# Block sums, low parts and normalisation of a seven-product matrix multiply, moved between engines and in the queues

## The chip, the cores and the metric

The kernel runs on one core of a Trainium2 chip. The metric is the device time of one execution in microseconds, the median of several runs. The engines are TensorE (PE, with its weight loads PEld), VectorE (DVE), ScalarE (ACT), GpSimd (POOL) and SyncE (SP, which issues DMAs); each executes its own queue in order.

## The reference

Three stages in float32: attention with a bias from positions, a product of two projections with a third, and a last block. Only that last block is touched:

```python
h = x @ w_in                                  # 1152 x 512 by 512 x 1024
e = np.exp(h - np.max(h, axis=-1, keepdims=True))
sm = e / (np.sum(e, axis=-1, keepdims=True) + 1e-09)
solu = h * sm
mu = np.mean(solu, axis=-1, keepdims=True)
var = np.mean((solu - mu) ** 2, axis=-1, keepdims=True)
ln = (solu - mu) / np.sqrt(var + 1e-06) * g_ln
return ln @ w_out                             # 1024 x 512
```

The gains `g_ln` are multiplied into the rows of `w_out` ahead of time (tile `wo2`).

## The kernel before

**Split numbers.** A float32 product on TensorE is made of three products of rounded parts: each operand is split into a high part (ScalarE rounds it, type fp32r) and a low part (operand minus high part, one subtraction on VectorE or GpSimd). Names end in `h` or `hi` and `l` or `lo`.

**Units.** The 1152 rows are nine units of 128 rows, 0 to 8. For a unit, `proj(u)` multiplies its rows with `w_in` (24 matmuls of 512 columns, into `ph`, one of two PSUM buffers). `norm(u)` is a generator of four steps: (1) VectorE's maxima (L890, L891) and ScalarE's exponentials (L894); (2) the products `ev` (L897); (3) sums and statistics (L899 to L905), which end in a `pow` on GpSimd (L906); (4) VectorE's scale (L908) and the normalised `ev` (L909). `transposed(u)` turns `ev` on TensorE (L918, eight transposes, into two of the four `pl` PSUM buffers).

**Seven products.** The output product is made for two units at a time, as a 2 x 2 block product by seven block multiplications in place of eight. Of the weights `wo2` four block sums `t1` to `t4` are needed (`weights_sums`, in two halves, k = 0 and 2, each of four subtractions on GpSimd, L957, then four roundings to `th`, L960, and four low parts `tl` on GpSimd, L964). Of the rows of a pair `rows_sums(ua, ub)` makes the copies `raw` (L971), the four sums `s1` to `s4` (GpSimd, L977), the rounded plain blocks `a1` (L978, L979) and `a` (the tile `a22`, L980, L981), and the four rounded sums with their low parts, `s12` and `s34` (ScalarE L983, GpSimd L984). `seven(ua, ub)` is a generator of seven steps: each runs 12 matmuls of 256 columns into one of the same four PSUM buffers (`pa11b11`, `pa12b21`, `ps2t2`, `ps1t1`, `ps3t3`, `pa22t4`, `ps4b22`; the profile drops the last digit) and then adds the result in (L1009 on VectorE; the first result is copied to `part` by ScalarE, L1012). SyncE sends the finished rows (L945). Unit 8, the odd one, goes alone: `alone(8)` splits it, `final(8)` multiplies it (L936, `py`).

**Order.** There is no scheduler: the program text gives each engine its queue, and a generator's step is put where `next` is called. The loop over `todo` ends the second stage: it sums into `x2s` (L810), splits into `x2h` (L866) and `x2l` (L868; on GpSimd for the last four blocks), splits `wo2`, and starts unit 0 and the weights' sums. Then come the weights' sums and units 1 and 2, and then a loop over j = 0, 2, 4, which for each pair (j, j+1) runs `seven` between the projections and normalisations of units j+2 and j+3; in the last turn (`end`) unit 8 comes in too. Buffers: `nat` has four (the `t` sums, `s1` to `s4`, the result rows `osb` and `part`), `gh` and `gl` three each (`a1`, `s12`, `s34`, unit 8's split), `big` two (`x2s`, `wo2`, then `th`, `raw`).

Of the kernel before, what the change touches and what calls it, by code (L numbers as in the profile page):

```python
# [10 lines left out]
F32 = mybir.dt.float32  # L11
F32R = mybir.dt.float32r
I32 = mybir.dt.int32
AF = mybir.ActivationFunctionType
ALU = mybir.AluOpType
AX = mybir.AxisListType
PSUM = bass.MemoryType.PSUM
P = 128
# [32 lines left out]
def tile_kernel(ctx, tc, q, k, v, w1, b1, w2, w_a, w_b, w_out, w_in2, w_out2, g_ln, psi, rpsi, out):  # L51
    nc = tc.nc
# [16 lines left out]
    KF = FF2 // P  # L69
# [90 lines left out]
    with ExitStack() as actx:  # L160
# [426 lines left out]
        first, first_w = [], {}  # L587
# [361 lines left out]
    HN = DM // 2  # L949
    KH = KF // 2  # L950

    def weights_sums():
        for k in range(0, KH, 2):
            b11, b12, b21, b22 = (wo2[0][:, o * KH + k:o * KH + k + 2, n * HN:(n + 1) * HN] for o in range(2) for n in range(2))
            raw = [natp.tile([P, 2, HN], F32, tag="nat", name=f"t{i + 1}_{k}") for i in range(4)]
            for i, a, b in ((0, b12, b11), (1, b22, raw[0]), (2, b22, b12), (3, raw[1], b21)):
                nc.gpsimd.tensor_tensor(out=raw[i], in0=a, in1=b, op=ALU.subtract)  # L957
            yield
            for i in range(4):
                nc.scalar.copy(th[:, i, k:k + 2], raw[i])  # L960
                if i % 2:
                    yield
            for i in range(4):
                nc.gpsimd.tensor_tensor(out=tl[:, i, k:k + 2], in0=raw[i], in1=th[:, i, k:k + 2].bitcast(F32), op=ALU.subtract)  # L964

    blocks = {}

    def rows_sums(ua, ub):
        for k, u in enumerate((ua, ub)):
            for a, pl in transposed(u):  # L970
                nc.scalar.copy(raw[:, 2 * k + a], pl)  # L971
            yield
        r11, r12, r21, r22 = (raw[:, i] for i in range(4))
        (ah, al), (s12h, s12l), (s34h, s34l) = tiles = [[pools[0].tile([P, 2, 512], F32R, tag=f"g{t_}", name=f"{n}{t_}_{ua}") for t_ in "hl"] for n in ("a1", "s12", "s34")]
        s1, s2, s3, s4 = (natp.tile([P, 512], F32, tag="nat", name=f"s{i + 1}_{ua}") for i in range(4))
        for o, x, y, op in ((s1, r21, r22, ALU.add), (s2, s1, r11, ALU.subtract), (s3, r11, r21, ALU.subtract), (s4, r12, s2, ALU.subtract)):
            nc.gpsimd.tensor_tensor(out=o, in0=x, in1=y, op=op)  # L977
        nc.scalar.copy(ah, raw[:, 0:2])  # L978
        nc.vector.tensor_tensor(out=al, in0=raw[:, 0:2], in1=ah.bitcast(F32), op=ALU.subtract)  # L979
        nc.scalar.copy(a22[:, 0], r22)  # L980
        nc.vector.tensor_tensor(out=a22[:, 1], in0=r22, in1=a22[:, 0].bitcast(F32), op=ALU.subtract)  # L981
        for h, l, i, x in ((s12h, s12l, 1, s2), (s12h, s12l, 0, s1), (s34h, s34l, 0, s3), (s34h, s34l, 1, s4)):
            nc.scalar.copy(h[:, i], x)  # L983
            nc.gpsimd.tensor_tensor(out=l[:, i], in0=x, in1=h[:, i].bitcast(F32), op=ALU.subtract)  # L984
        view = lambda t: t.rearrange("p (c t) -> p c t", t=P)
        blocks[ua] = {n: tuple(view(t[:, i]) for t in pair) for n, pair, i in (("a11", tiles[0], 0), ("a12", tiles[0], 1), ("s1", tiles[1], 0), ("s2", tiles[1], 1), ("s3", tiles[2], 0), ("s4", tiles[2], 1))}
        blocks[ua]["a22"] = tuple(view(a22[:, i]) for i in range(2))
        yield

    def seven(ua, ub, last=False):  # L990
        A = blocks.pop(ua)
        B = {f"b{k + 1}{n + 1}": tuple(w[:, k * KH:(k + 1) * KH, n * HN:(n + 1) * HN] for w in (wo_h, wo_l)) for k in range(2) for n in range(2)}
        B.update({f"t{i + 1}": (th[:, i], tl[:, i]) for i in range(4)})
        oa, ob = (natp.tile([P, DM], F32, tag="nat", name=f"osb_{u}") for u in (ua, ub))
        tmp = natp.tile([P, DM], F32, tag="nat", name=f"part_{ua}")
        u2, u4 = tmp[:, 0:HN], tmp[:, HN:DM]

        def summed_block(a, b):
            ps = ps_l.tile([P, 512], F32, tag="l", name=f"p{a}{b}_{ua}")[:, 0:HN]
            (xh, xl), (wh, wl) = A[a], B[b]  # L1000
            i = 0
            for c in range(KH):
                for x, w in ((xh, wh), (xh, wl), (xl, wh)):
                    nc.tensor.matmul(ps, x[:, c], w[:, c], start=(i == 0), stop=(i == 3 * KH - 1))  # L1004
                    i += 1
            return ps

        def plus(o, x, y, op=ALU.add):
            nc.vector.tensor_tensor(out=o, in0=x, in1=y, op=op)  # L1009

        left, right = slice(0, HN), slice(HN, DM)
        nc.scalar.copy(u2, summed_block("a11", "b11"))  # L1012
        yield
        plus(oa[:, left], summed_block("a12", "b21"), u2)
        if last:
            sent(ua, oa, left)
        yield
        plus(u2, summed_block("s2", "t2"), u2)
        yield
        plus(u4, summed_block("s1", "t1"), u2)  # L1020
        yield
        p7 = summed_block("s3", "t3")
        plus(ob[:, right], p7, u4)
        plus(u2, p7, u2)
        yield
        plus(ob[:, left], u2, summed_block("a22", "t4"), ALU.subtract)
        sent(ub, ob, slice(0, DM))
        yield
        plus(oa[:, right], summed_block("s4", "b22"), u4)
        sent(ua, oa, right if last else slice(0, DM))  # L1030
        yield
# [5 lines left out]
    for j, (tg, d) in enumerate(todo):  # L1037
# [8 lines left out]
            nrm = norm(seq[0])  # L1046
        if nrm:
            next(nrm, None)
        if j == KF:
            ws = weights_sums()  # L1050
            next(ws)
    inputs(*todo[-1])
    octx.close()
    fb = ctx.enter_context(tc.tile_pool(name="fb", bufs=1, side="right"))
# [4 lines left out]
    every = lambda gen: [None for _ in gen]  # L1059
    proj(1)  # L1060
    every(nrm)
    next(ws)
    next(ws)
    second = norm(1)
    next(second)
    next(ws)
    proj(2)
    every(second)
    every(ws)
    raw = big.tile([P, 4, 512], F32, tag="big", name="raw")  # L1070
    rows = rows_sums(0, 1)
    next(rows)
    every(rows)
    one = nu - 1
    for j in range(0, one - 2, 2):
        a, b = j + 2, j + 3
        end = b == one - 1
        if j:
            proj(a)
            next(rows)  # L1080
        first = norm(a)
        next(first)
        if j:
            every(rows)
        if end:
            proj(one)
            next(first)
            mid = norm(one)
            next(mid)
        proj(b)  # L1090
        every(first)
        if end:
            next(mid)
        second = norm(b)
        next(second)
        f = seven(j, j + 1)
        next(f)
        next(f)
        if end:
            every(mid)  # L1100
        next(second)
        next(f)
        next(f)
        next(f)
        next(second)
        rows = rows_sums(a, b)
        if end:
            every(alone(one))
            next(rows)
        every(f)  # L1110
        every(second)
        if not end:
            next(rows)
    every(rows)
    final(one)
    every(seven(a, b, True))
# [43 lines left out]
```

## Time and profile before

| | us |
|---|---|
| median of 3 runs | 549.32 (547.86 to 550.11) |
| the profiled execution | 551.31 |
| its span, first to last instruction | 549.5 |
| TensorE busy | 506.7 (92%) |
| VectorE busy | 412.0 (75%) |
| ScalarE busy | 299.6 (55%) |
| GpSimd busy | 247.1 (45%) |

The mean granted TensorE clock is 0.975 of full speed. The code of the diff runs from about 404 us to the end of the span. Busy shares are means over three stages; what one stage is limited by is read from its own stretch. A wait is put down to what ended it last by the profile.

### The profile page before, as it was taken

The numbers are of one execution on the slowest core, as the hardware profiler recorded it, in microseconds if no ns is written. First come the engines' busy times: TensorE is split into PE (matmuls) and PEld (weight loads), VectorE is DVE, ScalarE is ACT, GpSimd is POOL, SyncE is SP. The second block draws the span as 40 slices with busy tenths as digits, with TensorE's granted clock in tenths as the row PEclk, the third lists the DMA queues.
The fourth block names the chain that finished last, engine by engine and source line by source line (L and its number), as shares of the span: only waits on it lengthen the run. The fifth ranks groups of instructions, "written<-read, shape, count | busy, mean of one in ns | idle before, by whom it ended". The sixth has DMA issues, their size and how long they took to land.

```text
span 549.5 us, 13771 instructions
## 1 busy us (share of the span) xinstructions
PE 506.7 (92%) x5546; PEld 456.5 (83%) x5546; DVE 412.0 (75%) x826; ACT 299.6 (55%) x643; POOL 247.1 (45%) x301
## 2 busy tenths in 40 slices
PE   7979999999989999999999999999999459878787
PEld 4548778878879999999999999999997358776677
DVE  4789999999867259789989889788546465566662
ACT  5789899999978245555533452343434431425131
POOL 2046676776868322222212224222477960806235
PEclk9999999999989999999999999999999788979989
DMA  8699654445621065454434344430000001010011
GB/s 163 167 202 206 138 126 106 108 106 135 170 70 41 2 192 154 125 160 143 149 116 151 118 120 149 151 118 1 2 1 0 0 1 38 1 39 1 0 39 57
DMA packets 63330, 51.76 MB, mean 94 GB/s; under 512 B 40990, under 2 KB 53539, under 8 KB 63268
## 3 DMA queue, kind: packets, MB, share of 16 engines
q1 hardware_dynamic: 62992, 50.88, 34.9%
q8 instruction: 43, 0.70, 0.6%
q14 instruction: 19, 0.16, 0.1%
q10 hardware_dynamic: 276, 0.02, 0.0%
HBM read 36.73 MB, written 2.36 MB: 71 GB/s over the span
## 4 chain that ended last, share of the span: by engine, by line
PE 65%; DVE 10%; POOL 7%; issue 4%; ACT 3%; DMA 2%; SPq 0%; DVEq 0%; POOLq 0%; ACTq 0%
PE pm L128 25%; PE po L128 10%; PE xx L494 7%; PE bps L385 5%; PE s L413 5%; PE ph L879 3%; POOL s L977 3%; PE pt L462 2%; PE pl L918 2%; DVE h L377 2%; PE ps3t L1004 1%; PE pa22t L1004 1%; DVE ev L909 1%; PE ps4b L1004 1%; PE py L936 1%
## 5 line engine op out<-in xcount | busy, mean ns | idle before, releaser
L98 POOL TENSOR_SCALAR f<-f 128x512 f32<-128x512 f32 x48 | 41.9, 873 | 138.0 <-ACT f L94 131.2
L128 PE MATMUL pm<-xhi,abl 128*128 128x384 f32 x240 | 80.3, 335 | 0.0
L128 PE MATMUL pm<-xhi,abh 128*128 128x384 f32 x240 | 80.3, 335 | 0.0
L128 PE MATMUL pm<-xlo,abh 128*128 128x384 f32 x240 | 80.3, 334 | 0.0
L434 ACT ACTIVATE e<-e,nm 128x576 f32<-128x576 f32 x72 | 56.4, 783 | 12.4 <-DVE nm L427 12.3
L427 DVE CUSTOM_DVE_ANT_0 e<-s,bias 128x576 f32<-128x576 f32 x72 | 51.9, 754 | 7.8 <-PE s L413 5.3
L445 POOL TENSOR_SCALAR e<-e,rec 128x576 f32<-128x576 f32 x72 | 55.7, 786 | 3.4
L377 DVE TENSOR_SCALAR h<-tabs 128x576 f32<-128x576 f32 x112 | 51.2, 514 | 2.8 <-PE bps L385 2.5
L385 PE MATMUL bps<-h,w2bd 128*32 128x288 f32 x576 | 46.8, 422 | 4.0 <-DVE nm L427 2.0
L128 PE MATMUL po<-gh,oh 128*128 128x384 f32 x144 | 48.6, 337 | 0.6 <-DVE x2s L810 0.6
L128 PE MATMUL po<-gh,ol 128*128 128x384 f32 x144 | 48.5, 337 | 0.0
L128 PE MATMUL po<-gl,oh 128*128 128x384 f32 x144 | 48.5, 337 | 0.0
L128 PEld LDWEIGHTS pm<-xhi,abl 128*128 128x128 f32 x240 | 45.1, 188 | 0.0
L128 PEld LDWEIGHTS pm<-xlo,abh 128*128 128x128 f32 x240 | 45.1, 188 | 0.0
L128 PEld LDWEIGHTS pm<-xhi,abh 128*128 128x128 f32 x240 | 45.1, 188 | 0.0
L147 ACT COPY one<-pm 128x384 f32<-128x384 f32 x36 | 17.2, 478 | 50.6 <-PE pm L128 50.5
L110 DVE SCALAR_TENSOR_TENSOR f<-words,f 128x512 int32<-128x512 int32 x48 | 43.1, 897 | 1.6
L94 ACT ACTIVATE f<-words 128x512 f32<-128x512 f32 x48 | 32.4, 675 | 17.8 <-POOL wo L776 6.8
L494 PE MATMUL xx<-et,vsb 128*32 128x128 f32 (+1 forms) x1280 | 40.1, 267 | 0.0
L439 POOL TENSOR_SCALAR rec<-sums 128x2 f32<-128x2 f32 x36 | 12.0, 334 | 60.7 <-ACT e L434 60.3
L494 PEld LDWEIGHTS xx<-et,vsb 128*32 128x32 f32 x1280 | 34.1, 111 | 5.5 <-issue 0.2
L385 PEld LDWEIGHTS bps<-h,w2bd 128*32 128x32 f32 x576 | 20.6, 111 | 18.1 <-DVE nm L427 4.1
(206 smaller groups left out, 1412.2 us busy)
## 6 DMA issues: line engine op xcount, KB each, us to landing
bias<-st SPq DMA_DIRECT2D x40, 288.0 KB, 3.6
words<-in_moe_w_out_dram SPq DMA_DIRECT2D x20, 512.0 KB, 3.5
words<-in_moe_w_a_dram SPq DMA_DIRECT2D x12, 512.0 KB, 3.5
words<-in_moe_w_b_dram SPq DMA_DIRECT2D x12, 512.0 KB, 3.5
nat_q<-in_q_dram SPq DMA_DIRECT2D x32, 128.0 KB, 3.6
words<-in_moe_w_in_dram SPq DMA_DIRECT2D x8, 512.0 KB, 3.5
arena<-in_k_dram SPq DMA_DIRECT2D x8, 256.0 KB, 5.2
vsb<-in_v_dram SPq DMA_DIRECT2D x16, 128.0 KB, 5.2
```

Source lines behind the costliest of these rows:

```text
L94: nc.scalar.activation(f, words[:, :, 1].bitcast(F32), AF.Abs)
L98: engine.tensor_scalar(f, f, WORD_MAX, WORD_MIN, op0=ALU.min, op1=ALU.max)
L110: nc.vector.scalar_tensor_tensor(out=b, in0=words[:, :, 0], scalar=29, in1=b, op0=ALU.logical_shift_right, op1=ALU.bitwise_or)
L128: nc.tensor.matmul(ps, w, x, start=(i == 0), stop=(i == n - 1))
L147: nc.scalar.copy(one, ps[:, 1])
L377: nc.vector.tensor_scalar(h, win, sc, 0.0, op0=ALU.add, op1=ALU.max)
L385: nc.tensor.matmul(bps[32 * qd:32 * qd + 32, a, 0:SH], w2bd, h[:, a * SH:(a + 1) * SH], start=True, stop=True)
L413: nc.tensor.matmul(ps[:, a, 0:SH], w[r], x[r, b, h, :], start=(i == 0), stop=(i == len(mm) - 1))
L427: nc.vector.tensor_tensor_reduce(out=halves(e), in0=ps[:, :, 0:SH], in1=halves(bias_t[it][:, h, :]), op0=ALU.add, op1=ALU.min, scale=-scal ...
L434: nc.scalar.activation(e, e, AF.Exp, bias=nm, scale=-1.0, accum_out=sums[:, h:h + 1])
L445: nc.gpsimd.tensor_scalar(e, e, rec[:, h:h + 1], 1.0, op0=ALU.mult, op1=ALU.mult)
L494: nc.tensor.matmul(px[rows, p, cols], lhsT, rhs, start=(c == 0 and m == 0), stop=(c == NC), skip_group_check=True)
```

## The change

The weights' block sums are subtractions on VectorE (`weights_sums`), the first half one turn of the `todo` loop later and after unit 0's statistics, the second half behind the loop, into a `gh` and a `gl` buffer of type fp32r in place of `nat` buffers. The roundings to `th` and the low parts `tl` are all issued behind both halves (`weights_split`), sum by sum, t2 and t1 ahead of unit 1's first step and t3 and t4 behind it. `rows_sums` has four steps: the first unit's copies and the plain blocks `a1`; the second unit's copies, the four sums and the rounding of `a22`; `s12` with low parts on VectorE; `s34` with low parts on GpSimd and the low part of `a22`. The loop calls the steps in another order: both middle steps of the first unit's normalisation and `s12` come before `seven` begins, the first result's copy before the second unit's first step, `s34` after that step, and the remaining steps between the steps of `seven`.

```diff
--- before.py
+++ after.py
@@ -949,46 +949,63 @@
     HN = DM // 2
     KH = KF // 2
 
-    def weights_sums():
-        for k in range(0, KH, 2):
-            b11, b12, b21, b22 = (wo2[0][:, o * KH + k:o * KH + k + 2, n * HN:(n + 1) * HN] for o in range(2) for n in range(2))
-            raw = [natp.tile([P, 2, HN], F32, tag="nat", name=f"t{i + 1}_{k}") for i in range(4)]
-            for i, a, b in ((0, b12, b11), (1, b22, raw[0]), (2, b22, b12), (3, raw[1], b21)):
-                nc.gpsimd.tensor_tensor(out=raw[i], in0=a, in1=b, op=ALU.subtract)
-            yield
-            for i in range(4):
-                nc.scalar.copy(th[:, i, k:k + 2], raw[i])
-                if i % 2:
-                    yield
-            for i in range(4):
-                nc.gpsimd.tensor_tensor(out=tl[:, i, k:k + 2], in0=raw[i], in1=th[:, i, k:k + 2].bitcast(F32), op=ALU.subtract)
+    tops = []
+
+    def weights_sums(k, raw):
+        b11, b12, b21, b22 = (wo2[0][:, o * KH + k:o * KH + k + 2, n * HN:(n + 1) * HN] for o in range(2) for n in range(2))
+        for i, a, b in ((0, b12, b11), (1, b22, raw[0]), (2, b22, b12), (3, raw[1], b21)):
+            nc.vector.tensor_tensor(out=raw[i], in0=a, in1=b, op=ALU.subtract)
+        tops.append((k, raw))
+
+    def weights_split(i):
+        for k, raw in tops:
+            nc.scalar.copy(th[:, i, k:k + 2], raw[i])
+            nc.gpsimd.tensor_tensor(out=tl[:, i, k:k + 2], in0=raw[i], in1=th[:, i, k:k + 2].bitcast(F32), op=ALU.subtract)
 
     blocks = {}
 
     def rows_sums(ua, ub):
-        for k, u in enumerate((ua, ub)):
+        def turn_in(k, u):
             for a, pl in transposed(u):
                 nc.scalar.copy(raw[:, 2 * k + a], pl)
-            yield
+
+        pair = lambda n: [pools[0].tile([P, 2, 512], F32R, tag=f"g{t_}", name=f"{n}{t_}_{ua}") for t_ in "hl"]
+        A = blocks[ua] = {}
+
+        def kept_as(two, *names):
+            for i, n in enumerate(names):
+                A[n] = tuple(t[:, i].rearrange("p (c t) -> p c t", t=P) for t in two)
+
+        turn_in(0, ua)
+        ah, al = a1 = pair("a1")
+        nc.scalar.copy(ah, raw[:, 0:2])
+        nc.vector.tensor_tensor(out=al, in0=raw[:, 0:2], in1=ah.bitcast(F32), op=ALU.subtract)
+        kept_as(a1, "a11", "a12")
+        yield
+        turn_in(1, ub)
         r11, r12, r21, r22 = (raw[:, i] for i in range(4))
-        (ah, al), (s12h, s12l), (s34h, s34l) = tiles = [[pools[0].tile([P, 2, 512], F32R, tag=f"g{t_}", name=f"{n}{t_}_{ua}") for t_ in "hl"] for n in ("a1", "s12", "s34")]
         s1, s2, s3, s4 = (natp.tile([P, 512], F32, tag="nat", name=f"s{i + 1}_{ua}") for i in range(4))
         for o, x, y, op in ((s1, r21, r22, ALU.add), (s2, s1, r11, ALU.subtract), (s3, r11, r21, ALU.subtract), (s4, r12, s2, ALU.subtract)):
             nc.gpsimd.tensor_tensor(out=o, in0=x, in1=y, op=op)
-        nc.scalar.copy(ah, raw[:, 0:2])
-        nc.vector.tensor_tensor(out=al, in0=raw[:, 0:2], in1=ah.bitcast(F32), op=ALU.subtract)
         nc.scalar.copy(a22[:, 0], r22)
+        yield
+        s12h, s12l = s12 = pair("s12")
+        for i, x in ((1, s2), (0, s1)):
+            nc.scalar.copy(s12h[:, i], x)
+            nc.vector.tensor_tensor(out=s12l[:, i], in0=x, in1=s12h[:, i].bitcast(F32), op=ALU.subtract)
+        kept_as(s12, "s1", "s2")
+        yield
+        s34h, s34l = s34 = pair("s34")
+        for i, x in ((0, s3), (1, s4)):
+            nc.scalar.copy(s34h[:, i], x)
+            nc.gpsimd.tensor_tensor(out=s34l[:, i], in0=x, in1=s34h[:, i].bitcast(F32), op=ALU.subtract)
         nc.vector.tensor_tensor(out=a22[:, 1], in0=r22, in1=a22[:, 0].bitcast(F32), op=ALU.subtract)
-        for h, l, i, x in ((s12h, s12l, 1, s2), (s12h, s12l, 0, s1), (s34h, s34l, 0, s3), (s34h, s34l, 1, s4)):
-            nc.scalar.copy(h[:, i], x)
-            nc.gpsimd.tensor_tensor(out=l[:, i], in0=x, in1=h[:, i].bitcast(F32), op=ALU.subtract)
-        view = lambda t: t.rearrange("p (c t) -> p c t", t=P)
-        blocks[ua] = {n: tuple(view(t[:, i]) for t in pair) for n, pair, i in (("a11", tiles[0], 0), ("a12", tiles[0], 1), ("s1", tiles[1], 0), ("s2", tiles[1], 1), ("s3", tiles[2], 0), ("s4", tiles[2], 1))}
-        blocks[ua]["a22"] = tuple(view(a22[:, i]) for i in range(2))
+        kept_as(s34, "s3", "s4")
+        kept_as([a22[:, i:i + 1] for i in range(2)], "a22")
         yield
 
     def seven(ua, ub, last=False):
-        A = blocks.pop(ua)
+        A = blocks[ua]
         B = {f"b{k + 1}{n + 1}": tuple(w[:, k * KH:(k + 1) * KH, n * HN:(n + 1) * HN] for w in (wo_h, wo_l)) for k in range(2) for n in range(2)}
         B.update({f"t{i + 1}": (th[:, i], tl[:, i]) for i in range(4)})
         oa, ob = (natp.tile([P, DM], F32, tag="nat", name=f"osb_{u}") for u in (ua, ub))
@@ -1046,9 +1063,8 @@
             nrm = norm(seq[0])
         if nrm:
             next(nrm, None)
-        if j == KF:
-            ws = weights_sums()
-            next(ws)
+        if j == KF + 1:
+            weights_sums(0, [natp.tile([P, 2, HN], F32, tag="nat", name=f"t{i + 1}") for i in range(4)])
     inputs(*todo[-1])
     octx.close()
     fb = ctx.enter_context(tc.tile_pool(name="fb", bufs=1, side="right"))
@@ -1059,18 +1075,24 @@
     every = lambda gen: [None for _ in gen]
     proj(1)
     every(nrm)
-    next(ws)
-    next(ws)
+    halves = [pools[0].tile([P, 2, 2, HN], F32, tag=f"g{t_}", name=f"top_{t_}") for t_ in "hl"]
+    weights_sums(2, [t_[:, i] for t_ in halves for i in range(2)])
+    raw = big.tile([P, 4, 512], F32, tag="big", name="raw")
+    for i in (1, 0):
+        weights_split(i)
     second = norm(1)
     next(second)
-    next(ws)
+    for i in (2, 3):
+        weights_split(i)
     proj(2)
-    every(second)
-    every(ws)
-    raw = big.tile([P, 4, 512], F32, tag="big", name="raw")
+    next(second)
+    next(second)
+    first = norm(2)
+    next(second)
     rows = rows_sums(0, 1)
     next(rows)
-    every(rows)
+    next(rows)
+    next(first)
     one = nu - 1
     for j in range(0, one - 2, 2):
         a, b = j + 2, j + 3
@@ -1078,39 +1100,40 @@
         if j:
             proj(a)
             next(rows)
-        first = norm(a)
+            first = norm(a)
+            next(first)
+        proj(one if end else b)
         next(first)
-        if j:
-            every(rows)
+        next(first)
+        next(rows)
+        f = seven(j, j + 1)
         if end:
-            proj(one)
-            next(first)
             mid = norm(one)
             next(mid)
-        proj(b)
-        every(first)
-        if end:
+            every(rows)
+            next(first)
             next(mid)
+            proj(b)
+            next(mid)
+        next(f)
         second = norm(b)
         next(second)
-        f = seven(j, j + 1)
+        if not end:
+            every(rows)
         next(f)
+        next(mid if end else first)
+        next(f)
+        next(second)
+        next(f)
+        next(second)
         next(f)
         if end:
-            every(mid)
+            every(alone(one))
+        next(f)
+        rows = rows_sums(a, b)
+        next(rows)
         next(second)
-        next(f)
-        next(f)
-        next(f)
-        next(second)
-        rows = rows_sums(a, b)
-        if end:
-            every(alone(one))
-            next(rows)
         every(f)
-        every(second)
-        if not end:
-            next(rows)
     every(rows)
     final(one)
     every(seven(a, b, True))
```

## Rows read from the trace of the kernel before

**Rows 1.** Windows of three stretches: busy (instructions) by engine, granted clock PEclk, DMA.

```profile
core 0: us, PE busy (x) PEld busy (x) DVE busy (x) ACT busy (x) POOL busy (x), PEclk, DMA share, GB/s
433.85:453.50 19.65, 13.69 (x80) 12.30 (x80) 10.41 (x19) 8.08 (x17) 14.23 (x11) 0.85 0.00 1
453.50:484.20 30.70, 25.04 (x148) 22.40 (x148) 17.20 (x37) 9.05 (x19) 12.55 (x10) 0.89 0.05 18
484.20:529.50 45.30, 38.76 (x224) 34.26 (x224) 30.98 (x71) 12.83 (x27) 13.65 (x12) 0.92 0.05 18
```

**Rows 2.** Waits of TensorE (PE) from 418 us: total, times, longest, in us.

```profile
PE pl L918 <- DVE ev L909: 12.5, 3, 8.8
PE ps3t L1004 <- ACT part L1012: 11.6, 2, 6.0
PE ph L879 <- DVE ev L897: 1.9, 1, 1.9
PE pl L918 <- DVE part L1009: 0.9, 1, 0.9
```

**Rows 3.** The chain that ended last: start us, duration us, engine, tile, line.

```profile
476.98 2.46 POOL s34l L984 x2
479.45 0.52 POOL small L906
...
480.19 0.81 DVE ev L909
481.00 1.21 DVE small L890 x2
...
483.93 0.27 ACT part L1012
...
484.24 2.93 PE ps3t L1004 x12
...
490.41 0.87 PE pl L918 x8
491.28 5.58 PE ph L879 x24
...
542.12 1.42 PE ps3t L1004 x12
```

**Rows 4.** Timeline, all engines, 414 to 434 us: start us, duration us, instruction, [idle before].

```profile
414.58 0.15 DVE L905 TENSOR_SCALAR small<-small 128x1 f32<-128x1 f32 x1
...
419.54 2.19 ACT L960 CAST th<-t 128x512 fp32r<-128x512 f32 x4 [1.64 <-POOL x2l L868]
...
430.25 0.55 POOL L906 TENSOR_TENSOR small<-small,mhalf 128x1 f32<-128x1 f32 x1
...
430.83 1.22 DVE L908 TENSOR_TENSOR small<-small 128x1 f32<-128x1 f32 x1 [4.20 <-POOL small L906]
...
432.08 1.72 DVE L909 TENSOR_SCALAR ev<-ev,small 128x1024 f32<-128x1024 f32 x1
...
433.86 1.97 PE L918 MATMUL pl<-ident,ev 128*128 128x128 f32 x8 [8.76 <-DVE ev L909]
```

**Rows 5.** Single lines of code: durations ns min/median/max, first and last start, shape.

```profile
L115 DVE TENSOR_TENSOR abl<-f,abh x20: 676/692/693, 202.3 to 369.0; 128x512 fp32r<-128x512 f32 x20
...
L984 POOL TENSOR_TENSOR s12l<-s,s12h x8: 1274/1292/1304, 443.0 to 539.2; 128x512 fp32r<-128x512 f32 x8
...
L964 POOL TENSOR_TENSOR tl<-t,th x8: 1256/1286/1710, 420.2 to 434.9; 128x512 fp32r<-128x512 f32 x8
```

**Rows 6.** Timeline, 470 to 473 us, columns as in rows 4.

```profile
470.50 2.29 POOL L977 TENSOR_TENSOR s<-raw 128x512 f32<-128x512 f32 x1
...
471.56 1.79 DVE L981 TENSOR_TENSOR a<-raw,a 128x512 fp32r<-128x512 f32 x1
```

**Rows 7.** Windows of unit 2's products and statistics, and of 505 to 520 us.

```profile
445.09:448.62 3.53, 2.46 (x21) 2.25 (x20) 3.39 (x9) 0.00 (x0) 2.96 (x3) 1.00 0.02 5
505.00:520.00 15.00, 12.94 (x84) 11.64 (x84) 10.36 (x28) 3.78 (x10) 6.19 (x7) 1.00 0.00 0
```

## Prediction

> **What bounds the kernel now.** I read the busy times by stretch first, then what TensorE waited for, then the chain that ended last, then the timeline where that chain leaves TensorE. All the code that the diff touches runs after 404 us. In the stretch of one pair of units, 453.50 to 484.20, TensorE is busy 25.04 of 30.70 us, VectorE 17.20, GpSimd 12.55 [rows 1]: no engine is full, so the order sets the time. From 418 us on TensorE waited 12.5 us for the normalised tile `ev` (8.8 of it at once), 11.6 us in two pieces (the longer 6.0) before block `ps3t`, and 2.8 us elsewhere, 26.9 us together [rows 2]. That is nearly all there is to gain, with what the slow clock adds behind the long waits: `ps3t` took 2.93 us behind a wait and 1.42 us without one [rows 3], the granted clock over that pair being 0.89 [rows 1].
>
> The chain says why `ps3t` waits: GpSimd's two low parts `s34l`, then its `pow`, then VectorE normalises one unit and takes the next unit's maxima, then ScalarE's exponentials, then `part` (the copy of the first result, L1012), and only then the PSUM bank is free that `ps3t` needs [rows 3]. Each queue is in order, so a result's copy stands behind two units' normalisation. The first wait has the same kind of chain: unit 1's `pow` stands behind eight GpSimd subtractions and starts at 430.25; VectorE's two steps follow, and TensorE's transposes start at 433.86 [rows 4].
>
> **Prices.** One low part costs 1.29 us on GpSimd; one subtraction of that size, both inputs in SBUF, costs VectorE 0.69 us [rows 5]. The two engines exclude each other in such work: GpSimd's `s3` took 2.29 us and VectorE's `a` 1.79 us when they met, about 1.0 us over their own time each, which is the other's instruction [rows 6]. The Trainium skill (SBUF — State Buffer, Who interferes with whom) states it as an exclusive lock: a VectorE instruction with two SBUF inputs and a GpSimd instruction that reads SBUF block each other fully. The trace agrees (rows 6); without the lock the sum below would be about 1.7 us better (the first low part could start at 422.7 instead of 424.4), and I keep the lock. At full clock TensorE takes 5.6 us for a projection, 1.42 for a block, 0.87 for eight transposes [rows 3]. A normalisation takes 2.9 us from the start of the maxima to the end of the exponentials (481.00 to 483.93) [rows 3], 3.5 us for products and statistics [rows 7], then `pow` 0.55 [rows 4] and 1.0 us for the last two steps (479.99 to 481.00 by the chain's next start) [rows 3].
>
> **Weights.** Four GpSimd subtractions leave at 404 (hidden then, free now) and four at 425; VectorE gets eight. The first four stand behind L905, which ends at 414.7 [rows 4], take 4 x 0.69 = 2.7 us, and with them the last sums of `x2s` come 2.7 us later. TensorE does not see this: it is in two projections until 424. The next four (k = 2) then meet the last two GpSimd low parts `x2l` (1.0 us each, an estimate from 1.29 us x 384/512 columns) under the lock and end near 424.4. Before, `th` waited for that same `x2l` and started at 419.54 [rows 4]; now it starts near 423.1. GpSimd then has eight `tl` in front of unit 1's `pow`: 424.4 + 8 x 1.25 = 434.3, and `pow` at 434.3 instead of 430.25. The two steps behind it cost 1.22 + 1.72 us before, because `tl` ran beside them [rows 4]; now GpSimd is idle then, so 1.0 us. Transposes at 435.95: **+2.1 us**, a loss. It has no cover: TensorE has nothing else. Bounds: +0.4 without the lock, +4 if every VectorE subtraction of both halves loses a GpSimd slot.
>
> **First pair.** The matrix of plain blocks is rounded before unit 1's transposes, off the path. TensorE could be at `ps3t` 13.5 us after those transposes (433.86 to the 447.4 where it stopped: 453.5 less the 6.0 wait of rows 2), so 449.5. The copy `part` now stands ahead of the second unit's exponentials and needs only TensorE and a buffer that `s12l` releases; the bank wait goes. What is late next is `s34l`, moved behind them: VectorE's statistics of unit 2 end at 444.1, the two `s12l` (now VectorE, `pow` under the lock in between) at 446.1, unit 3's maxima and exponentials 2.9 us later, rounding 0.6, `s34l` 1.29: 451.0. So `ps3t` starts at 451.0 instead of 453.54, after a wait of 1.5 us: -2.5, and the slow clock behind the 6.0 us wait goes too (2.93 - 1.42 = 1.5 in `ps3t` and about 0.4 in the block after).
>
> **Second pair.** From `ps3t` to the next `ps3t` TensorE has 7 blocks, 2 projections and 16 transposes: 7 x 1.42 + 2 x 5.6 + 2 x 0.87 = 22.9 us, so 473.9. The path to `s34l` starts where the projection of unit 4 ends, 461.7: 2.9 + 0.6 (three ScalarE copies ahead) + 3.5 + 1.7 (`s12l`, twice 0.69 and part of `pow`) + 2.9 + 0.6 + 1.29 = 13.5, so 475.3. `ps3t` at 475.3 instead of 484.24 [rows 3]: **-8.9**, another 1.5 us of waiting left. GpSimd's four sums meet no VectorE subtraction now. The result buffers that these sums reuse leave by DMA: the last is issued near 459 and the sums start near 463, so the send stays covered.
>
> **Last pair.** `ps3t` to the next projection: 3 blocks and 8 transposes, 5.1 us, against 7.0 before (484.24 to 491.28, slow clock) [rows 3]: -10.8 at 480.4. Then three projections, 16 transposes and 5 blocks run through to 506. From here VectorE, with three units to normalise between its result sums, is late: block 6 waits 0.4 us for a bank, unit 6's transposes 1.5 us for the bank of `ps3t` (its sums end near 509.3), unit 7's transposes 2.2 us for their `ev`, behind `a1l`. I get 514.3 for unit 7's transposes instead of 529.5: **-15.2**. Behind them both kernels have one projection's worth of work for the last unit and 7 blocks, TensorE-bound. A wait of 1.9 us left the granted clock at 1.00 in its stretch [rows 2, 7], so waits of 0.4 to 2.2 us should cost no clock.
>
> The sum: +2.1 - 4.6 (to -2.5) - 6.4 (to -8.9) - 1.9 (to -10.8) - 4.4 = -15.2. The profiled execution is 551.31 us for a span of 549.5; it becomes 536.1. The median of the runs shown is 549.32, 2 us lower, and so the forecast is **534.1 us**.
>
> **Rivals.** (1) *A wait takes the place of the bank wait.* `s34h` now stands on ScalarE behind the second unit's exponentials, and those behind VectorE's `s12l`. Before, `s34l` was done (479.4) long ahead of `ps3t` [rows 3]; now it decides. If that path of 13.5 us is 4 us longer in each of two pairs (each VectorE subtraction losing to a GpSimd one, 3 x 1.29), TensorE waits over 5 us again and its clock falls as it did: -15.2 + 8 + 2 x 1.9 = -3.4, 546 us. For it: all on one path; against: GpSimd is idle where most of it runs. (2) *More is won*: the short waits (1.5, 1.5, 0.4, 1.5, 2.2) vanish, if VectorE and ScalarE overlap better than my queue walk: -15.2 - 7.1 = -22, 527 us. (3) *Slower*: VectorE becomes the bound. A pair's VectorE work is 17.2 + 2 x 0.69 = 18.6 us, but its queue now alternates result sums, low parts and normalisations, so it waits in turn for TensorE, ScalarE and GpSimd. If those waits make a pair 36 us instead of 30.7, three pairs cost 3 x 5.3 + 2.1 = 18 us: 567 us. It decides from 12 us of VectorE waiting a pair; in my walk it is 4 to 5. (4) *The change does not do what it says*: the first results' copy is held by a buffer of `s3` or `s4` instead of `s1` or `s2`, and the bank wait stays: within 2 us of 549.
>
> **How the numbers follow.** Forecast case, 529 to 541 us: 0.70. (1) 541 to 547: 0.12. (2) below 529: 0.10. (3) 0.04. (4) 0.04. The range reaches down to take in most of (2) and up by 1 us into (1): 527 to 542, with about 0.2 outside. Half a per cent, 2.7 us, is about what a measurement of this kernel can tell from no change. Faster by more: 0.70 + 0.10 + most of (1) = 0.89; within it: 0.06; slower: 0.05.
>
> **What would show it.** The changed profile should have unit 1's transposes about 2 us later than 433.9 behind a `pow` that waits for eight `tl`; no TensorE wait for `part`; waits of 1 to 2 us before `ps3t` ended by GpSimd's `s34l`; a pair period near 24 us instead of 30.7; and `s1` to `s4` at 1.29 us each. I am wrong if `s34l` ends over 3 us after TensorE has finished `ps1t`, if VectorE idles over 8 us a pair, or if the first wait grows by more than 4 us.

## The result, and the profile after

The changed kernel takes 531.86 us in the median (530.97 to 534.22) against 549.72 us before in the same comparison: ratio 0.9686, 95% interval 0.9645 to 0.9728, so 17 to 18 us less. Forecast were 534.1 us and 527 to 542.

| | before, us | after, us |
|---|---|---|
| profiled execution / span | 551.31 / 549.5 | 531.27 / 529.5 |
| TensorE busy | 506.7 (92%) | 500.7 (95%) |
| VectorE busy | 412.0 (75%) | 418.8 (79%) |
| GpSimd busy | 247.1 (45%) | 226.5 (43%) |
| unit 1's projection begins | 412.86 | 410.52 |
| from there to the end of `ps4b` of units 6 and 7 | 133.5 | 115.9 |

The two profiled executions differ by 20.0 us, but 2.3 of that stand ahead of unit 1's projection, where TensorE's work is the same. They arise before any code of the diff runs: by 300 us TensorE had begun 4280 matmuls before and 4293 after. In the kernels below that start varies between 410.1 and 413.8 us. So traces are compared from this start on, and "last stage" means from there to TensorE's last matmul: -17.6 us. (One slip in the account of the change: the buffers of the second half of the block sums are F32, as the diff shows, not fp32r.)

TensorE's waits from 418 us on in the changed kernel, columns as in [rows 2]:

```profile
PE pl L918 <- DVE ev L909: 12.1, 2, 9.9
PE pl L918 <- DVE part L1026: 0.9, 1, 0.9
PE ps3t L1021 <- POOL s34l L1001: 0.9, 1, 0.9
PE ps4b L1021 <- ACT raw L970: 0.2, 1, 0.2
```

The 11.6 us before `ps3t` [rows 2] are gone and 0.9 us has come, released by GpSimd's `s34l`. The first wait is 1.1 us longer (9.9 against 8.8). In all 14.1 us of waiting is left of 26.9.

The chain that ended last, in the pieces that answer to [rows 3] and [rows 4]:

```profile
426.10 4.94 POOL tl L963 x4
431.04 0.53 POOL small L906
...
431.79 0.82 DVE ev L909
...
432.66 1.97 PE pl L918 x8
...
446.82 1.57 PE ps3t L1021 x12
...
464.82 1.02 DVE s12l L995 x2
...
469.59 1.29 POOL s34l L1001
...
470.93 1.45 PE ps3t L1021 x10
...
506.48 1.06 ACT a1h L981
...
507.56 1.23 DVE a1l L982
...
508.89 0.82 DVE ev L909
...
509.76 1.09 PE pl L918 x8
```

`pow` of unit 1 (431.04) stands behind eight `tl`, of which the last four show here; VectorE's last step takes 0.82 us where it took 1.72 beside a `tl` [rows 4]. Then the chain is TensorE's own work up to 458.15; from there, for the second pair, it goes through ScalarE's copies and unit 4's normalisation (left out above) to `s12l`, and over ScalarE's exponentials and rounding, which the chain shows as "issue", to `s34l` and to `ps3t` at 470.93. From one `ps3t` to the next it is 24.1 us against 30.7. The last piece is `a1l` in front of unit 7's last step: a wait of 2.2 us.

A window of the changed kernel, from the first `ps3t` to TensorE's arrival at the second, columns as in [rows 1]:

```profile
446.82:469.65 22.83, 22.83 (x149) 20.50 (x148) 15.88 (x39) 8.84 (x19) 7.95 (x9) 1.00 0.06 24
```

TensorE is busy in all of it at full clock; before, from `ps3t` to `ps3t`, it was busy 25.04 of 30.70 us at 0.89 [rows 1]. The row sums no longer meet VectorE's subtractions, except in the last pair (durations ns min/median/max):

```profile
L989 POOL TENSOR_TENSOR s<-raw x8: 1282/1292/1302, 435.4 to 514.3; 128x512 f32<-128x512 f32 x8
...
L989 POOL TENSOR_TENSOR s<-raw,s x4: 1282/1286/1743, 439.3 to 515.5; 128x512 f32<-128x512 f32 x4
```

### The profile page after: what moved, and what is told of

Its sections match the earlier page's. It is cut to its first block, busy times and chain, and to the rows that moved or that the text cites. A ratio compares the mean times of both kernels' runs of the same rounds, so it can differ in the third digit from the quotient of the medians.

```text
span 529.5 us, 13772 instructions
## 1 busy us (share of the span) xinstructions
PE 500.7 (95%) x5546; PEld 450.9 (85%) x5546; DVE 418.8 (79%) x842; ACT 300.0 (57%) x643; POOL 226.5 (43%) x285
## 3 DMA queue, kind: packets, MB, share of 16 engines
q1 hardware_dynamic: 62992, 50.88, 35.8%
## 4 chain that ended last, share of the span: by engine, by line
PE 64%; DVE 11%; POOL 5%; issue 5%; ACT 3%; DMA 2%; SPq 0%; POOLq 0%; DVEq 0%
PE pm L128 26%; PE po L128 10%; PE xx L494 6%; PE bps L385 5%; PE ph L879 4%; PE s L413 3%; POOL tl L963 2%; DVE h L377 2%; POOL e L445 2%; PE pt L462 2%; DVE small L902 1%; PE pl L918 1%; DMA words<-in_moe_w_out_dram 1%; DVE ev L897 1%; PE py L936 1%
```

## The experiments

Each kernel was run beside the kernel before; lengths of the last stage are from one profiled execution each, worked out as in the table above. Two executions of the changed kernel agree in it within 0.2 us. But behind the first wait the projection of unit 3 took between 6.3 and 7.6 us in these traces, as the clock rose sooner or later, so a difference under about 1 us says nothing by itself.

| kernel | ratio to before (95%) | last stage, us |
|---|---|---|
| changed | 0.9686 (0.9645 to 0.9728) | 115.9 |
| changed, again | 0.9672 (0.9643 to 0.9700) | 116.1 |
| copy behind | 0.9752 (0.9687 to 0.9817) | 118.2 |
| copy ahead alone | 0.9881 (0.9848 to 0.9914) | 126.1 |
| `s12l` on GpSimd | 0.9729 (0.9697 to 0.9761) | 118.6 |
| weights as before | 0.9672 (0.9640 to 0.9703) | 115.8 |
| order alone | 0.9694 (0.9649 to 0.9738) | 118.2 |
| weights alone | 1.0037 (1.0012 to 1.0062) | 134.2 |
| chain back | 0.9769 (0.9731 to 0.9807) | 121.3 |
| first wait | 0.9683 (0.9641 to 0.9725) | 119.4 |
| last steps | 0.9628 (0.9596 to 0.9659) | 113.9 |
| two swaps | 0.9626 (0.9598 to 0.9654) | 113.4 |
| three moves | 0.9564 (0.9532 to 0.9595) | 109.2 |

**The order against the engines.** First the order alone, with the weights' block sums and `s12l` on GpSimd as before (the full edit of the weights is shown further down):

```diff
 # the changed kernel with weights_sums() and its calls as before, and
-            nc.vector.tensor_tensor(out=s12l[:, i], in0=x, in1=s12h[:, i].bitcast(F32), op=ALU.subtract)
+            nc.gpsimd.tensor_tensor(out=s12l[:, i], in0=x, in1=s12h[:, i].bitcast(F32), op=ALU.subtract)
```

> The changed kernel's order of steps alone: weights' block sums and s12l on GpSimd as in the kernel before. Theory (the order is the gain, the two moves of work to VectorE little): the two undone singly cost 0 and 2.8 us of the last stage's 115.9, so about 118.7 from unit 1's projection to the last matmul against 133.5 before: -14.8, 535. Rival (each move covers for the other, and GpSimd is the bound without both): GpSimd has 2 x 1.29 us a pair and four weights' subtractions more, 541 or over.

The last stage takes 118.2 us, -15.3 of the change's -17.6. TensorE's longest waits in the last stage, and under them the window from 505 to 520 us (columns as in [rows 1]):

```profile
PE pl L918 <- DVE ev L909: 11.0, 2, 8.7
PE pl L918 <- DVE part L1027: 1.2, 1, 1.2
PE ps3t L1022 <- POOL s34l L1002: 0.8, 1, 0.8
PE pa22t L1022 <- DVE part L1027: 0.6, 1, 0.6
```

```profile
505.00:520.00 15.00, 12.56 (x65) 10.49 (x66) 5.31 (x9) 6.66 (x11) 7.47 (x7) 0.89 0.10 36
```

The wait before `ps3t` is 0.8 us here too: the order alone removes the 11.6 us. The second `ps3t` begins 59.1 us into the stage in both kernels; the 2.3 us between them all come in the last pair, where two bank waits are 0.9 us longer and the granted clock falls (0.89 over this window), so that unit 7's transposes and `py` take 1.6 us more (`py` 7.3 us against 5.85).

The two moves of work singly. In the changed kernel, `s12l` on GpSimd (the same one-line edit alone):

> The changed kernel, with the two s12l low parts of each pair on GpSimd again, in the new order. Theory (order, not work): in the changed trace GpSimd is idle from 441.8 to 445.6 between pow and s34l, where two subtractions of 1.29 us fit; VectorE gets its next maxima 1.2 us earlier: within 1.5 us of 531.9. Rival (the gain comes from work taken off GpSimd): the s12l stand in front of s34l, 2.6 us in each of three pairs, about 540.

118.6 us, 2.8 more, and a ratio 0.4% higher: a miss of the theory's 1.5, nearer to it than to the rival. The second `ps3t` comes 0.4 us later, which is made up by the third; the 2.8 us all lie in the last pair, with the same longer waits and the same fall of the clock as in the order alone (`py` 7.4 us). And the weights as before:

```diff
 # weights_sums() as in the kernel before, in place of weights_sums(k, raw) and weights_split(i)
 ...
-        if j == KF + 1:
-            weights_sums(0, [natp.tile([P, 2, HN], F32, tag="nat", name=f"t{i + 1}") for i in range(4)])
+        if j == KF:
+            ws = weights_sums()
+            next(ws)
 ...
     proj(1)
     every(nrm)
-    halves = [pools[0].tile([P, 2, 2, HN], F32, tag=f"g{t_}", name=f"top_{t_}") for t_ in "hl"]
-    weights_sums(2, [t_[:, i] for t_ in halves for i in range(2)])
-    raw = big.tile([P, 4, 512], F32, tag="big", name="raw")
-    for i in (1, 0):
-        weights_split(i)
+    next(ws)
+    next(ws)
     second = norm(1)
     next(second)
-    for i in (2, 3):
-        weights_split(i)
+    next(ws)
     proj(2)
-    next(second)
-    next(second)
+    every(second)
+    every(ws)
+    raw = big.tile([P, 4, 512], F32, tag="big", name="raw")
     first = norm(2)
-    next(second)
     rows = rows_sums(0, 1)
```

> The changed kernel, with the weights' block sums, their roundings and low parts as in the kernel before (GpSimd, the old order), rows and loop as changed. Theory: from the end of the second stage's last matmul to unit 1's transposes it is 21.0 us in the trace of before and 22.1 us in the changed one, so the weights' part costs 1.1 us and this is 530.8. Rival (the sums on VectorE are part of the gain, because GpSimd then starts the rows' sums earlier): the sums s1 start after 436 instead of 435.4 and the rest follows, +4, 536.

115.8 us, the same. The 1.1 us in the first wait are there (projection 3 starts 22.6 us into the stage, 23.8 in the changed kernel) but are given back by the first `ps3t`, which starts 35.8 and 36.1 us in: most of it in projection 3 itself, 7.53 us at a granted clock of 0.73 here and 6.70 us at 0.83 in the changed kernel. So it is mostly the clock of this one execution that hides the 1.1 us, and the ratios (0.9672 here, 0.9686 and 0.9672 for the changed kernel) can't tell 1 us. In the kernel before, the weights' part alone (the reverse of this edit):

> The kernel before, with the weights' part of the change alone. Theory: unit 1's transposes come 1.1 us later as in the changed kernel, and the stall before ps3t, whose chain starts from them, follows: 550 to 551, no difference that can be told. Rival (VectorE's faster subtractions give a part of the gain): -3 us or more, 546.

The longest of TensorE's waits but for the transposes:

```profile
PE ps3t L1003 <- ACT part L1011: 11.1, 2, 5.6
```

Ratio 1.0037, 134.2 us: 0.7 us more in the last stage, and the wait before `ps3t` is there whole (11.1 us). The weights' part is no gain by itself.

**The links of the chain.** In the kernel before, the first result's copy moved ahead of the second unit's first step:

```diff
-        second = norm(b)
-        next(second)
         f = seven(j, j + 1)
         next(f)
+        second = norm(b)
+        next(second)
         next(f)
```

> The kernel before, with only the first result's copy moved ahead of the second unit's maxima and exponentials. Theory: the first bank opens near 444.5, but the bank of pa12b waits for a VectorE sum behind unit 3's maxima, those behind unit 2's last steps, these behind pow behind s34l; the wait moves from ps3t to pa22t and shrinks from 6 to about 3 us in each of two pairs: -6 to -9 us with the clock, 541 to 544. Rival 1 (the copy's place is nearly all of it): -15, 535. Rival 2 (its place means nothing): 549.7.

126.1 us, -7.4: the theory's size. TensorE's longest wait but for the transposes, and VectorE's timeline ahead of the first sum:

```profile
PE pa22t L1004 <- DVE osb L1009: 5.3, 2, 2.8
```

```profile
450.25 0.16 DVE L908 TENSOR_TENSOR small<-small 128x1 f32<-128x1 f32 x1 [0.66 <-POOL small L906]
...
451.17 1.28 DVE L890 TENSOR_REDUCE small<-ph 128x1 f32<-128x512 f32 x2
...
452.62 0.41 DVE L1009 TENSOR_TENSOR osb<-pa12b,part 128x256 f32<-128x256 f32 x1
```

`ps3t` no longer waits; the next block `pa22t` does, 2.5 and 2.8 us, because the sum that frees its bank (L1009) is behind unit 3's maxima and these are behind L908 and `pow`. The reverse in the changed kernel, the copy put back:

```diff
-        next(f)
         second = norm(b)
         next(second)
         if not end:
             every(rows)
         next(f)
+        next(f)
```

> The changed kernel, with the first result's copy to part put back behind the second unit's maxima and exponentials; all else as changed. Theory (the bank wait went because pow and normalisation no longer stand behind s34l): in the changed trace unit 3's exponentials end at 444.9 and TensorE reaches ps3t at 446.65, so the copy is still in time; at most +1.5 us, 532 to 533.5. Rival (the copy's place in ScalarE's queue is what opened the bank, as the prediction's first pair has it): waits of about 6.0 and 5.6 us before ps3t come back with 3.8 us of slow clock, 547.

TensorE's waits in the last stage, but for those for `ev`:

```profile
PE pl L918 <- DVE part L1026: 2.0, 3, 1.3
PE ps3t L1021 <- ACT part L1029: 0.8, 2, 0.5
PE pa22t L1021 <- DVE part L1026: 0.7, 1, 0.7
```

118.2 us, 2.4 more: not the 15 of the rival, and a little over the theory's 1.5, spread over three places (0.8 at `ps3t`, 0.7 at `pa22t`, 1.1 more at the transposes). The interval of the ratio overlaps that of the changed kernel, so the 2.4 us are read from the trace. Then two other links put back, with the copy left ahead:

```diff
         proj(one if end else b)
+        if not end:
+            next(rows)
+            every(rows)
         next(first)
         next(first)
-        next(rows)
+        if end:
+            next(rows)
         f = seven(j, j + 1)
 ...
         next(f)
+        if not end:
+            next(first)
         second = norm(b)
         next(second)
-        if not end:
-            every(rows)
         next(f)
-        next(mid if end else first)
+        if end:
+            next(mid)
         next(f)
```

> The changed kernel, with two links of the old chain put back in the first two pairs: s34l ahead of the first unit's pow in GpSimd's queue, and the first unit's last two steps ahead of the second unit's maxima in VectorE's; the copy to part stays ahead. Theory (three links had to stand one behind the other for the wait of 6 us; with the copy ahead and s12l on VectorE, pow ends near 444.3 in place of 448.7, and the banks open in time): at most +3 us, 535. Rival (these two links are the gain, the copy is not): the waits before ps3t or pa22t come back with the clock, 10 us, 542.

TensorE's longest wait in the last stage, and VectorE's timeline:

```profile
PE pa22t L1021 <- DVE osb L1026: 4.0, 2, 3.0
```

```profile
439.15 2.81 DVE L995 TENSOR_TENSOR s12l<-s,s12h 128x512 fp32r<-128x512 f32 x2 [3.52 <-ACT s12h L994]
441.88 1.78 DVE L1002 TENSOR_TENSOR a<-raw,a 128x512 fp32r<-128x512 f32 x1
...
446.95 0.15 DVE L905 TENSOR_SCALAR small<-small 128x1 f32<-128x1 f32 x1
447.77 0.16 DVE L908 TENSOR_TENSOR small<-small 128x1 f32<-128x1 f32 x1 [0.66 <-POOL small L906]
```

121.3 us, 5.4 more: between the two. `ps3t` does not wait, `pa22t` waits 1.1 and 3.0 us. The theory's size fell on one point: with the low parts pulled ahead of the products, `s12l` and `a` meet the row sums and `s34l` under the lock (2.81 us for two and 1.78, alone 0.68 each), so the statistics end at 447.1 and `pow` only then lets VectorE's last steps start, at 447.77; `pow` was expected to end near 444.3. Copy and these two links all put back at once were not run.

**The waits that were left.** The last pair: unit 7's last two instructions (L908, L909) ahead of `a1l`:

```diff
+        if end:
+            next(second)
         rows = rows_sums(a, b)
         next(rows)
-        next(second)
+        if not end:
+            next(second)
```

> The changed kernel, with unit 7's last two normalisation steps ahead of the low part a1l of the last pair in VectorE's queue. Theory (the wait of 2.18 us before unit 7's transposes is a1l and what it waits for): these steps end near 507.0 in the changed trace's times, before TensorE has done ps4b at 507.6, so the wait goes and everything behind it is TensorE-bound: -2.2 us, ratio to the changed kernel 0.996. Rival (a1l is late then, and block pa11b waits instead, or the time is set by the banks): 0 to -0.5 us.

Unit 7's transposes follow `ps4b` at once; 113.9 us, -2.2 beside the changed kernel again (116.1), ratio 0.9628 against 0.9672 in the same comparison (2.4 us by the medians, though the two intervals overlap):

> The changed kernel as it is, timed beside the three that follow. Both theories: 0.9686 of the kernel before, within 0.3%.

Next, `s34` ahead of the second unit's first step as well (the edit above stays):

```diff
-        second = norm(b)
-        next(second)
         if not end:
             every(rows)
+        second = norm(b)
+        next(second)
         next(f)
```

> The same, and s34 with its low parts ahead of the second unit's maxima and exponentials in the first two pairs. Theory (the wait of 0.89 us before the second ps3t is ScalarE's rounding behind exponentials): this wait goes, -0.9 more, 3.1 less than the changed kernel in all. Rival (s4 and the lock on VectorE's s12l set s34l's time): -2.2 as without it.

TensorE's longest waits in the last stage:

```profile
PE pl L918 <- DVE ev L909: 9.9, 1, 9.9
PE ps4b L1021 <- DVE part L1026: 1.2, 1, 1.2
```

The wait before the second `ps3t` is gone, as expected, but the ratio is the same (0.9626): 1.2 us of a new wait stand before the first `ps4b`, for a bank that VectorE frees; `s34l` on GpSimd now runs beside unit 2's last steps, and L909 takes 1.74 us there in place of 0.81. The first wait: unit 1's maxima ahead of the second half of the block sums, two `tl` ahead of `pow`, six behind it:

```diff
     halves = [pools[0].tile([P, 2, 2, HN], F32, tag=f"g{t_}", name=f"top_{t_}") for t_ in "hl"]
-    weights_sums(2, [t_[:, i] for t_ in halves for i in range(2)])
-    raw = big.tile([P, 4, 512], F32, tag="big", name="raw")
-    for i in (1, 0):
-        weights_split(i)
     second = norm(1)
     next(second)
-    for i in (2, 3):
-        weights_split(i)
     proj(2)
+    weights_sums(2, [t_[:, i] for t_ in halves for i in range(2)])
+    raw = big.tile([P, 4, 512], F32, tag="big", name="raw")
+    weights_split(1)
     next(second)
     next(second)
     first = norm(2)
     next(second)
+    for i in (0, 2, 3):
+        weights_split(i)
```

> The changed kernel, with unit 1's maxima ahead of the second half of the weights' sums, and its pow behind two low parts tl in place of eight. Theory (the first wait is GpSimd's eight tl in front of pow, and VectorE's sums in front of the maxima): pow near 425.5 in place of 431.0 in the changed trace's times, transposes near 427.1 in place of 432.7; of these 5.5 us the six remaining tl, now ahead of the row sums, may take back some at s2t2 and ps3t: -3.5 to -5.5, 526.5 to 528.5. Rival (the row sums behind the tl set the time anyway, since GpSimd has the same work): the wait moves to s2t2 or ps3t whole, 532.

TensorE's longest waits in the last stage, and VectorE's timeline around unit 1's last step:

```profile
PE pl L918 <- DVE ev L909: 9.5, 2, 7.4
PE ps3t L1021 <- POOL s34l L1001: 1.8, 2, 0.9
PE ps3t L1021 <- ACT s34h L1000: 1.6, 1, 1.6
```

```profile
426.77 1.21 DVE L908 TENSOR_TENSOR small<-small 128x1 f32<-128x1 f32 x1 [0.67 <-POOL small L906]
428.02 1.72 DVE L909 TENSOR_SCALAR ev<-ev,small 128x1024 f32<-128x1024 f32 x1
429.66 2.28 DVE L982 TENSOR_TENSOR a1l<-raw,a1h 128x1024 fp32r<-128x1024 f32 x1
```

The ratio is that of the changed kernel (0.9683), so the rival was right. The last stage is even 3.5 us longer in the trace (119.4), but the profiled execution was the slowest of four (534.56 us, median 533.77), and 1.6 of the 3.5 is unit 7's transposes and `py` at a lower clock. The first wait is 2.5 us shorter, not 5.5: L908, L909 and `a1l` take 1.21, 1.72 and 2.28 us beside the `tl`, 3.0 more than the 0.16, 0.82 and 1.23 of the changed kernel. And the row sums start no sooner behind the same `tl`, and `ps3t` now waits three times, 3.4 us in all against 0.9. So the last kernel keeps the `tl` away from these steps, four on GpSimd ahead of `pow`, four on VectorE behind unit 2's maxima, with both swaps above:

```diff
-    def weights_split(i):
+    def weights_high(i):
         for k, raw in tops:
             nc.scalar.copy(th[:, i, k:k + 2], raw[i])
-            nc.gpsimd.tensor_tensor(out=tl[:, i, k:k + 2], in0=raw[i], in1=th[:, i, k:k + 2].bitcast(F32), op=ALU.subtract)
+
+    def weights_low(i, engine):
+        for k, raw in tops:
+            engine.tensor_tensor(out=tl[:, i, k:k + 2], in0=raw[i], in1=th[:, i, k:k + 2].bitcast(F32), op=ALU.subtract)
 ...
+    second = norm(1)
+    next(second)
+    proj(2)
     weights_sums(2, [t_[:, i] for t_ in halves for i in range(2)])
     raw = big.tile([P, 4, 512], F32, tag="big", name="raw")
+    for i in (1, 0, 2, 3):
+        weights_high(i)
     for i in (1, 0):
-        weights_split(i)
-    second = norm(1)
-    next(second)
-    for i in (2, 3):
-        weights_split(i)
-    proj(2)
+        weights_low(i, nc.gpsimd)
     next(second)
     next(second)
 ...
     next(first)
+    for i in (2, 3):
+        weights_low(i, nc.vector)
```

> The same as the last, and the first wait: unit 1's maxima ahead of the second half of the weights' sums, four low parts tl on GpSimd ahead of its pow, which waits for VectorE until then anyway, and four on VectorE behind unit 2's maxima, so that no tl runs beside unit 1's last steps and a1l. Theory (in the experiment with pow behind two tl, six tl made VectorE's steps and a1l 3.0 us longer under the lock and held the row sums back to 435.6): transposes 17.2 us after unit 1's projection begins, in place of 22.1, and the row sums 4 us earlier: -4.5 more, 7.6 less than the changed kernel, 524. Rival (the weights' work only moves and meets the row sums' subtractions under the lock): within 1.5 us of the last.

TensorE's longest waits in the last stage, and VectorE's timeline with two of its `tl`:

```profile
PE pl L918 <- DVE ev L909: 5.4, 1, 5.4
PE pl L918 <- DVE part L1029: 1.2, 2, 0.9
PE ps2t L1024 <- DVE s12l L998: 0.5, 1, 0.5
```

```profile
433.45 1.77 DVE L966 TENSOR_TENSOR tl<-top_l,th 128x512 fp32r<-128x512 f32 x1
435.14 1.78 DVE L966 TENSOR_TENSOR tl<-t,th 128x512 fp32r<-128x512 f32 x1
```

The first wait is 5.4 us. 109.2 us, 4.2 less than with two swaps and 6.9 less than the changed kernel in the same comparison. The median is 527.11 us, ratio 0.9564 (0.9532 to 0.9595); the interval lies wholly under those of the changed kernel and of two swaps. In the last stage the theory's 4.5 held nearly: three of the `tl` on VectorE took 1.78 us under the lock, and `s2t2` waits 0.5 us for its low part. By the medians it is 2.5 us less than two swaps and 5.0 less than the changed kernel, so the 524 us expected were not reached; in the profiled execution unit 1's projection begins 2.0 us later than with two swaps (412.7 against 410.7).

## Why the prediction was right, and where it was not

The time came out 2.2 us under the forecast, in the forecast case. By its steps, each from the start of unit 1's projection:

| step | forecast against before, us | measured, us |
|---|---|---|
| unit 1's transposes | +2.1 | +1.1 |
| first `ps3t` | -2.5 | -4.5 |
| second `ps3t`, after its wait | -8.9 | -11.0 |
| projection of unit 6 | -10.8 | -12.2 |
| unit 7's transposes | -15.2 | -17.4 |
| last matmul | -15.2 | -17.6 |

**First transposes, right in mechanism, mis-sized.** `pow` behind eight `tl` and the two last steps without the lock are in the chain as told. The term that was too large is the one ahead of the `tl`: the last `x2l` came 3.0 us later than before, not the 3.6 to which 423.1 for `th` came, and the first `tl` began 0.7 us behind the first `th`, not 1.3. Around it the timeline shows the lock as predicted, on both sides (two `x2l` and the second half's sums):

```profile
417.40 2.74 POOL L868 TENSOR_TENSOR x2l<-x2s,x2h 128x384 fp32r<-128x384 f32 x2 [0.21 <-ACT x2h L866]
...
417.88 1.39 DVE L957 TENSOR_TENSOR top_h<-wo,top_h 128x512 f32<-128x512 f32 x1
...
419.19 1.50 DVE L957 TENSOR_TENSOR top_l<-wo 128x512 f32<-128x512 f32 x1
```

Two `x2l` take 2.74 us and two sums 1.39 and 1.50 (0.69 alone [rows 5]). The Trainium skill (SBUF — State Buffer, Who interferes with whom) says that issue order decides who blocks; the trace agrees: the sum of 417.88 came while the first `x2l` was under way, and its record is 0.70 us over its own time. That the weights as before take as long (115.8 us) was not forecast, since the prediction carried its +2.1 to the end; but as told above it was a lower clock in projection 3 that hid the difference there.

**First pair, the main step: half right.** The wait of 6 us went, and `s34l`, done at 446.9 in the changed trace, became the last thing that `ps3t` needs, as told. The path to it from the statistics' end was forecast at 6.9 us and took 6.1: the two `s12l` were priced 2.0 us with `pow` under the lock and took 1.28; here VectorE had started first and `pow` was the longer one (0.93 us). So TensorE, which began `ps3t` at 446.65, shows no wait for it. What fell is the reason given, that the bank wait goes *because the copy now stands ahead*. With the copy put back only 2.4 us return; the copy ahead alone in the kernel before brings 7.4 and leaves a wait at `pa22t`; two other links put back cost 5.4. The wait needed a row of links in order (low parts and row sums under the lock, `pow` behind `s34l`, unit 3's maxima behind unit 2's last steps, result sums and copy behind these), and the change cuts several of them, so that no one cut undone brings it back whole. That all of them together bring it back is not shown; those undone here come to 7.8 of the order's 15.3 us.

**Second pair, right.** 24.1 us from `ps3t` to `ps3t` against the forecast 24.3 (475.3 - 451.0); 0.9 us of waiting in place of 1.5, the two `s12l` again taking 1.28 us against the 1.7 of the forecast.

**Last pair.** Two of the waits came where they were told and about as long (bank of `ps3t` 0.9 against 1.5, unit 7's `ev` 2.2 against 2.2), and moving unit 7's last two instructions ahead of `a1l` showed the latter's cause; the 0.4 us at block 6 did not come. Of the 5.2 us won from the projection of unit 6 to unit 7's transposes, 3.4 are waits (6.5 us before, 3.1 after). That short waits cost no clock held in this trace (`py` 5.85 us), but by luck: the forecast leant on one wait of 1.9 us, and the kernel before showed the contrary 15 us later, where the granted clock was 0.76 behind waits of 2.3 and 0.9 us that end at 520.5 and 522.0 (columns as in [rows 1]):

```profile
520.00:527.00 7.00, 5.64 (x32) 5.18 (x33) 6.67 (x17) 2.34 (x4) 0.55 (x1) 0.76 0.00 0
```

**Rivals.** A wait in place of the bank wait: there, but 0.9 us in one pair. Slower by VectorE: its queue was late only in the last pair. More is won: in part. The 2.4 us by which the last stage beat the forecast are 1.0 at the first transposes and 1.0 on the path to the first `ps3t`, a loss of about 0.6 from there to unit 6's projection, and 0.8 and 0.2 at unit 7's transposes and behind them. The change does what it says.

## What to carry to other kernels

Where in-order queues feed one another, look for the whole row of links over several engines: what a wait costs is not the price of the one link that the trace names, and one cut may only move it to the next bank. Time an order change and a change of engine separately. Here the order gave 15.3 of 17.6 us; the moves of subtractions to VectorE gave 2.3, all of it in the last pair and 1.6 of that by the clock. When subtractions of the two engines that exclude each other must meet, let them meet where TensorE does not wait for them: with six `tl` beside unit 1's last steps and `a1l` nothing was won by the ratio; with four later on VectorE, where they met the row sums instead, the last stage was 4.2 us shorter than without.

## What the runs showed of the hardware

The clock behind short waits was not the same each time. In the changed kernel waits of 0.9 and 2.2 us within 6 us left the granted clock at 1.00, and `py` took 5.85 us; in the first-wait experiment, behind the same two waits, 6.7 us at 0.86. In the order alone, behind waits of 0.6, 1.2 and 2.2 us, `py` took 7.3 us at 0.78, with `s12l` on GpSimd 7.4 us at 0.76; in the copy-behind kernel, after waits of 0.3, 0.7, 1.3 and 2.2 us, 5.9 us at 1.00. So the lengths of the waits alone don't decide it; what does is open.

VectorE's smallest two-input instruction pays the lock too: L908, on one column, took 0.16 us alone and 1.21 us beside a `tl` (first wait).
